# Prefix and suffix products by scans: reset by a maximum with a PSUM constant and four pad columns, in place of an added tile; the attention output moves to the first score bank

## The chip, the cores and the metric

One NeuronCore of a Trainium2 chip runs the whole kernel. The metric is the device time of one execution in microseconds (us); each run shown is one execution, and the median of several is compared. The engines are called as the profile calls them: PE (TensorE, matrix multiplication; PEld is its weight load), DVE (VectorE), ACT (ScalarE), POOL (GpSimd) and SP (SyncE, which issues the DMAs here). [...]

## The reference

A gated linear attention over 4 batches, 8 heads, 768 tokens and a head size of 48 feeds an MLP with a rational activation, 384 to 2048 to 384:

```python
for t in range(S):
    state = alpha[:, :, t, :, None] * state + einsum('bhd,bhe->bhde', k[:, :, t], v[:, :, t])
    y[:, :, t] = einsum('bhd,bhde->bhe', q[:, :, t], state)
...
h = x @ w_in                      # x: y with the heads joined, 3072 x 384
P = a[0] + a[1] * h + a[2] * h**2 + a[3] * h**3
Q = 1.0 + abs(b[0]) * abs(h) + abs(b[1]) * h**2
out = (P / (Q + 1e-06)) @ w_out
```

alpha is drawn between 0.8 and 1. All is float32, and matrix products in the later part of the kernel are split into a high and a low part (`gh` and `gl`, `hi` and `lo`).

## The kernel before

**Attention.** The tokens are cut into 24 chunks g of 128. Within a chunk the recurrence is turned into matrix products: k is multiplied by the product of all alphas after its token, q by the product of those up to it divided by the chunk's total. Both products come from DVE scans over a tile `ta` of shape 128 x 516: heads and channels on partitions, four groups side by side in the free dimension, each with one pad column and 128 tokens (`C1 = C + 1`). The step `suf` (line 404) runs backwards and gives `tg`, the step `pre` (line 419) runs forwards and gives `fp`. Each computes state = state * ta + second tile. The pad of `ta` is 0, which ends the group before; the second tile, 0 but in the pads, adds the start value of the next group: a constant 1 in `ones1` for `suf`, and in `d1` for `pre` the reciprocal of the chunk's total, which the steps `max` (line 409, clamps the total) and `inv` (line 416) put there just before. Both scans so read two SBUF tiles of 516 columns.

```python
nc.vector.tensor_tensor_scan(
    fp[g % 2], ta[g % 2][:, 0 : NC4 * C1], d1, 0.0, op0=ALU.mult, op1=ALU.add
)
```

Steps of one chunk, in the names of the order table: `ta`, `tk`, `tq` (DVE transposes of alpha, k and q into place; the first four chunks come by PE transposes `tn` and ACT copies `cp` instead), `suf`, `max`, `inv`, `pre`, `k` and `q` (multiply by the products, lines 433 and 436), `tot` (totals per head for the state, line 424), `s` (scores on PE into PSUM banks 4 and 5, line 450), `se` and `sm` (ACT copy, POOL mask, lines 457 and 461), `kt` and `ke` (k transposed on PE into bank 4, ACT copy), `d` (decay of the state, line 474), `am` (on PE: y into bank 3, and the new k-v products into bank 5, lines 492 and 511), `kv` (state update on DVE, lines 519 and 524), `xh` and `xl` (y out of its bank as a high part by ACT, line 538, and a low part by DVE, line 543).

**MLP.** Blocks m of 256 tokens, and for each 8 slices of 256 hidden columns: 96 units u in all, of which the first 16 run in plain float32 while the weights are still being joined and split. A unit is: `in` twice (PE, line 571 or 577, into bank u % 3), ACT `ah`, `t1`, `q1`, POOL `qm` (line 593), DVE `t2`, `t3` (lines 604, 608), ACT `ars`, `sq` (lines 611, 614), DVE `p`, `t`, `g` (lines 618, 621, 627; with `g` the bank is free), ACT `gh`, then `gl` (line 634, on POOL or DVE), and `oh` twice and `ol` (PE, lines 652 and 662, into banks 6 and 7). Weight steps early in the run: `abs` on ACT, `sign` (lines 246 and 248), `low`, `join` on DVE, `hi` on ACT, `lo` (line 286, DVE or POOL).

**What sets the order.** All steps are registered with `add(name, engine, cost, function, arguments, after, ...)`. The order in which they are issued is written out in the table `ORDER`, a compressed list of step numbers, one order for all engines together. Where a step has an `alt`, the high bit of its number says that the alternative engine runs it. The costs do nothing when the kernel is built. The waits between engines follow from what the steps read and write.

**PSUM banks.** 0 to 2: hidden units. 3: y (`bank(3)` in `attn_mm`, `x_hi`, `x_lo`, and the verdict at the end). 4 and 5: scores, transposed k, k-v products. 6 and 7: the output. Before the first units the banks also hold the transposed first inputs (`NAT_BANKS`).

A step at the end sums up whether any alpha lies outside 0.75 to 1.05; only then would a general path (`general`) run, which doesn't run with these inputs.

Of the kernel before, what the change touches and what calls it, by code (L numbers as in the profile page):

```python
# [22 lines left out]
class Plan:  # L23
# [85 lines left out]
    'h>7!P|oM~-F<oA+PCnTp@OgLI|lXqC|}W!b1i)@Khd@EqkUiB({~7KB>jAE-`2Nr^?e`T&bRjs{czVQ=;+3}2EK!@8P?',
    'wq@B{rA-^h>k-GVv3u^;Dqxj}w{pXlfMj()rk@mZj=Z|m0iP(R6ccb!Ib@$-B;H`!-{`924Xa#Q?NA2y<^U+=TS0zb|7',  # L110
    '@EiOh-z8Y=7y7||iSO+W_@#cMAL5t!>HeVK<g>z1pA$y-fo{1U=4bd7{*d3|2ZiN=t$wCI?8mrEezR{MHq;&Q+x#rQ-L',
    'LdV{VJauj``z$w!iFm_?`ZQF95rI9ysYw`PIG)gt^oHiXY&f_%%MnO>)=#NPouf_E-H=zt&&(dq&*w&;2uh(}%iO{+2)',
    'MyTUiW*XM(M{=3f)dEvJ28NBeX{T+YK7lfbwuD|DB`u*PP8-L#a@W1>YKh^#9Z@uaTUkEPx!ERdEegDpXk<qR&bc6T)w',
    '}0Tf!w~n-htm%}kv{T?^*{g58-47pPIpdw1rap7M${66Kl&n&ML&(`5k%6@KC6E5ph+~cM$xan7(~?>E}3=@qG@s^o$Z',
    'opbY(3LF*Jpy)Kr>UapV-2U1Mr76-}dQHJujM*qTeTX${Sxxi!!@8cS<xPA#EvwWN-Bv%=DA86EEPXkM+Q`LvYg*LYeK',
    'GH3#=ttFw3meq_}S_^1BEvPeH@1T{|)l6DQ%V}#Z1?3>Kme=~)Kzl%GXsCs?tya*AT1h)-5pAO#wVn3SqFPzYKqGCeeY',
    'L%I(k9wjt7uj2r~P%bcG0fdRLep&9i#)af6z_GXoz;#u{uzz>s$@hFl{z+jvKE%p~uMPS{?@LI31!xwHM6OiP}PkX-l1',
    ';y<ve4*DbnGC+QMhq&;=AZq;78SeNP)-KNWQx%SqnI!*fo)Ag9H&=I;rkLyZJsM~dyj?~>cLwD*-U8Q?;ua44vdQxxbY',
    'CWT8^@PsSn>t(P=zcw*r}UN1*IT+qPwQH}t@refp40PsU+?Ncy`Zo4fnL-%x=tVJdcCCa^^qPLxj{GSA3dz^^sipl$NE',
    'ICjC`yA=?6Wc|1@IoUXSWWHGvBv1)ub@La<qF@KnDj29blS`c=Pazu=lu@NDFF<>0zT4K}I-iGwJ?b4?QX;DtsDk_H-N',  # L120
    '4Wb7xHAWCK_@S|aY(eZGSr8{k8T{1bK@j}X6hV&Qx8@2`1v!J%L7E_LkUNMMgbVTn;e)(EzF=UGHb@u557GzugA74|pk',
    'NRo7!dRg3Iz#*!a>F$VUQ@u6l4yv1Vu)L1Vw{lLGd6o2n$LDrGxB2iJ)ZgKP+N&Ed',
# [13 lines left out]
    (0, "a"): (0, 1), (0, "k"): (2, 3), (0, "q"): (6, 7),  # L136
# [4 lines left out]
GB = 3  # L141
# [13 lines left out]
def tile_gla_then_rational_mlp(ctx, tc, q, k, v, alpha, w_in, w_out, ca, cb, out):  # L155
# [34 lines left out]
    def bank(n, cols=BANK):  # L190
        return ps[:, n * BANK : n * BANK + cols]
# [104 lines left out]
    C1 = C + 1  # L296
# [15 lines left out]
    st_d = work.tile([P, H * D], F32, name="st_d")  # L312
# [6 lines left out]
    def set_ta(s):  # L319
        nc.gpsimd.memset(ta[s][:, 0 : NC4 * C1 + 1 : C1], 0.0)  # L320

    def set_d1():
        nc.gpsimd.memset(d1, 0.0)
# [677 lines left out]
```

## Time and profile before

| | |
|---|---|
| median of 3 runs | 573.96 us (573.42 to 574.5) |
| the profiled execution | 574.5 us |
| its span, first to last instruction | 572.8 us |
| mean granted clock of PE | 0.993 |
| instructions | 13516 |
| DVE scans | 48 in two lines, 24 each |

In the lines of the profile, L404 is line 404 of the kernel; an entry such as `x24: 1204/1226/2378` is a count and the shortest, median and longest duration in ns; `| 18.9, 1889 |` is busy time in us and mean duration in ns. A wait is written with who waited, for whom, the total in us, how often and the longest. Durations of an engine's instructions may overlap by a little, so busy time is a union and not the sum.

### The profile page before, as it was taken

The numbers are of one execution on the slowest core, as the hardware profiler recorded it, in microseconds if no ns is written. First come the engines' busy times: TensorE is split into PE (matmuls) and PEld (weight loads), VectorE is DVE, ScalarE is ACT, GpSimd is POOL, SyncE is SP. The second block draws the span as 40 slices with busy tenths as digits, with TensorE's granted clock in tenths as the row PEclk, the third lists the DMA queues.
The fourth block names the chain that finished last, engine by engine and source line by source line (L and its number), as shares of the span: only waits on it lengthen the run. The fifth ranks groups of instructions, "written<-read, shape, count | busy, mean of one in ns | idle before, by whom it ended". The sixth has DMA issues, their size and how long they took to land.

```text
span 572.8 us, 13516 instructions
## 1 busy us (share of the span) xinstructions
PE 533.6 (93%) x5170; PEld 480.9 (84%) x5170; DVE 523.5 (91%) x767; ACT 457.5 (80%) x773; POOL 351.6 (61%) x316
## 2 busy tenths in 40 slices
PE   5888999889999999999899999999999999999995
PEld 4766666666798999899799999998999899999894
DVE  3999999999999999999899999899898999888883
ACT  2667776657897887987799898988888888898893
POOL 3257368757787776767479576665665565564351
PEclk9989999999999999999999999999999999999998
DMA  9978735355654452235434342543153120020001
GB/s 263 302 214 221 216 76 145 85 148 134 155 154 118 104 142 60 50 92 121 108 85 118 90 98 62 121 103 89 43 128 87 40 68 1 1 80 2 28 1 33
DMA packets 120550, 59.94 MB, mean 105 GB/s; under 512 B 101792, under 2 KB 113056, under 8 KB 120480
## 3 DMA queue, kind: packets, MB, share of 16 engines
q1 hardware_dynamic: 120480, 59.02, 39.9%
q8 instruction: 42, 0.69, 0.5%
q14 instruction: 28, 0.23, 0.1%
HBM read 47.98 MB, written 4.72 MB: 92 GB/s over the span
## 4 chain that ended last, share of the span: by engine, by line
DVE 30%; PE 29%; ACT 13%; DMA 10%; SPq 9%; issue 7%; POOL 2%; DVEq 0%; ACTq 0%
PE ps L577 12%; PE ps L652 7%; SPq L354 7%; PE ps L662 4%; DVE t L604 4%; DVE t L608 4%; DVE ps L621 3%; DVE t L618 3%; DMA wo_words<-in_moe_w_out_dram 3%; DVE t L627 3%; DMA raw_k<-in_k_dram 2%; DMA raw_a<-in_alpha_dram 2%; ACT ps L611 2%; DVE tg L404 2%; ACT ps L614 2%
## 5 line engine op out<-in xcount | busy, mean ns | idle before, releaser
L577 PE MATMUL ps<-x,wi 128*128 128x256 f32 x1440 | 199.6, 284 | 8.3 <-DVE t L627 6.7
L577 PEld LDWEIGHTS ps<-x,wi 128*128 128x128 f32 x1440 | 187.2, 189 | 18.0 <-DVE t L627 12.6
L593 POOL TENSOR_TENSOR qm<-qm,ah 128x512 f32<-128x512 f32 x96 | 131.5, 1371 | 107.6 <-ACT qm L590 102.4
L652 PE MATMUL ps<-wo,gh 128*128 128x384 f32 x640 | 136.0, 343 | 1.0 <-ACT gh L630 0.7
L652 PEld LDWEIGHTS ps<-wo,gh 128*128 128x128 f32 x640 | 105.9, 188 | 4.4 <-ACT gh L630 1.6
L634 POOL TENSOR_TENSOR gl<-t,gh 128x512 fp32r<-128x512 f32 x58 | 77.3, 1333 | 49.4 <-ACT gh L630 33.0
L611 ACT ACTIVATE ps<-qm,one_eps 128x512 f32<-128x512 f32 x96 | 66.2, 689 | 32.4 <-DVE t L608 21.1
L618 DVE SCALAR_TENSOR_TENSOR t<-t,coef,ps 128x512 f32<-128x512 f32 x96 | 70.6, 736 | 15.6 <-ACT ps L614 15.0
L590 ACT ACTIVATE qm<-ah,bab 128x512 f32<-128x512 f32 x96 | 77.9, 813 | 6.7 <-DVE ps L621 5.7
L587 ACT ACTIVATE t<-ps,coef 128x512 f32<-128x512 f32 x96 | 74.2, 772 | 9.7 <-PE ps L577 3.2
L584 ACT ACTIVATE ah<-ps 128x512 f32<-128x512 f32 x96 | 56.8, 593 | 25.4 <-PE ps L577 8.9
L608 DVE SCALAR_TENSOR_TENSOR t<-t,coef,ps 128x512 f32<-128x512 f32 x96 | 70.6, 737 | 3.3 <-ACT ah L584 1.9
L604 DVE TENSOR_TENSOR t<-t,ps 128x512 f32<-128x512 f32 x96 | 64.7, 675 | 7.7 <-ACT t L587 5.1
L662 PE MATMUL ps<-wo,gl 128*128 128x384 f32 x320 | 69.7, 340 | 0.9 <-DVE gl L634 0.9
L627 DVE SCALAR_TENSOR_TENSOR t<-ps,t 128x512 f32<-128x512 f32 x96 | 65.7, 684 | 1.8
L621 DVE SCALAR_TENSOR_TENSOR ps<-qm,ps 128x512 f32<-128x512 f32 x96 | 65.8, 685 | 0.1
L614 ACT ACTIVATE ps<-ps 128x512 f32<-128x512 f32 x96 | 56.1, 584 | 1.8
L662 PEld LDWEIGHTS ps<-wo,gl 128*128 128x128 f32 x320 | 53.4, 188 | 1.6 <-DVE gl L634 1.1
L630 ACT ACTIVATE gh<-t 128x512 fp32r<-128x512 f32 x80 | 50.1, 628 | 5.0 <-DVE t L627 4.7
L571 PE MATMUL ps<-x,wi_words 128*128 128x256 f32 x192 | 47.8, 392 | 5.9 <-DVE t L627 5.5
L571 PEld LDWEIGHTS ps<-x,wi_words 128*128 128x128 f32 x192 | 36.2, 194 | 16.7 <-DVE t L627 8.7
L645 PE MATMUL ps<-wo_words,t 128*128 128x384 f32 x128 | 46.8, 490 | 1.2 <-DVE t L627 1.2
(97 smaller groups left out, 732.2 us busy)
## 6 DMA issues: line engine op xcount, KB each, us to landing
raw_a<-in_alpha_dram SPq DMA_DIRECT2D x160, 48.0 KB, 2.1
raw_k<-in_k_dram SPq DMA_DIRECT2D x160, 48.0 KB, 2.1
raw_q<-in_q_dram SPq DMA_DIRECT2D x160, 48.0 KB, 2.1
wi_words<-in_moe_w_in_dram SPq DMA_DIRECT2D x8, 768.0 KB, 6.3
wo_words<-in_moe_w_out_dram SPq DMA_DIRECT2D x8, 768.0 KB, 7.5
tv<-in_v_dram SPq DMA_DIRECT2D x24, 192.0 KB, 3.2
out_dram<-parts SPq DMA_DIRECT2D x24, 192.0 KB, 2.3
wr<-in_alpha_dram SPq DMA_DIRECT2D x18, 256.0 KB, 3.0
```

The lines of the kernel that those rows point to most:

```text
L571: nc.tensor.matmul(h, whole(("i", j))[:, kt * FU + ff, :], x[:, kt, 0, :], start=(kt == 0), stop=(kt == KT - 1),)
L577: nc.tensor.matmul(h, w(("i", j))[:, kt * FU + ff, :], x[:, kt, xp, :], start=(kt == 0 and n == 0), stop=(kt == KT - 1 and n == 2),)
L590: nc.scalar.activation(buf(s, "qm", u), buf(s, "ah", u), AF.Identity, bias=b0, scale=b1)
L593: nc.gpsimd.tensor_tensor(buf(s, "qm", u), buf(s, "qm", u), buf(s, "ah", u), op=ALU.mult)
L604: nc.vector.tensor_tensor(t, t, h_of(u), op=ALU.mult)
L608: nc.vector.scalar_tensor_tensor(t, t, a1, h_of(u), op0=ALU.add, op1=ALU.mult)
L611: nc.scalar.activation(h_of(u), buf(s, "qm", u), AF.Abs_reciprocal_sqrt, bias=one_eps)
L618: nc.vector.scalar_tensor_tensor(t, t, a0, h_of(u), op0=ALU.add, op1=ALU.mult)
L621: nc.vector.scalar_tensor_tensor(h_of(u), buf(s, "qm", u), 1.0 + 1e-6, h_of(u), op0=ALU.add, op1=ALU.mult)
L627: nc.vector.scalar_tensor_tensor(t, h_of(u), 2.0, t, op0=ALU.subtract, op1=ALU.mult)
L652: nc.tensor.matmul(o_of(tt), buf(s, "gh", u)[:, ff, tt * P : (tt + 1) * P], w(("o", j))[:, ff, :], start=(j == j0 and ff == 0 and w is hi) ...
L662: nc.tensor.matmul(o_of(tt), buf(s, "gl", u)[:, ff, tt * P : (tt + 1) * P], hi(("o", j))[:, ff, :], start=False, stop=(j == j1 and ff == F ...
```

## The change

The scans no longer add a second tile; they take the maximum with one constant: state = max(state * ta, FLOOR) with FLOOR = 2^-55. The constant is one PSUM column of bank 3, broadcast over the columns. Between two groups there now stand four pad columns (`PAD = 4`, so 528 columns for 516). In `ta` the pads are 2^55, 0, 2^55 and a last one: the 0 brings the state down to FLOOR, the 2^55 next to it brings it to 1, and the last pad, which `inv` fills with the reciprocal of the total, makes it the start value for `pre`. `max` writes to PSUM (`least_p`), `inv` reads it there and writes into `ta`; `max` now runs on DVE only and is ordered after the `inv` of the chunk before, where it was ordered after the `pre`. `totals` reads its two halves from PSUM where DVE runs it. The tiles `d1` and `ones1` and their fills on POOL go; a DVE fill of bank 3 (`set_consts`) and more pad fills in `set_ta` come.

Bank 3 thereby is taken by constants. y moves to bank 4 (`SCB`), the first score bank, so that `s` of a chunk is ordered after `xh` and `xl` of the chunk before; the verdict moves there too; k of the first block is transposed into banks 4 and 5, where it was 2 and 3.

The order table is a new one. Read out step by step, its counts by engine are these (the steps whose engine changes beside others that stay):

| step | before, DVE / POOL | after, DVE / POOL |
|---|---|---|
| `max` | 4 / 20 | 24 / 0 |
| `tot` | 5 / 15 | 11 / 9 |
| `gl` | 22 / 58 | 14 / 66 |
| `k` | 4 / 20 | 2 / 22 |
| `q` | 5 / 19 | 3 / 21 |
| `lo` | 5 / 11 | 2 / 14 |
| `sign` | 12 / 4 | 11 / 5 |
| `d` | 4 / 16 | 4 / 16, four others each way |

PE, ACT and SP run the same steps as before, in another order.

```diff
-    (0, "a"): (0, 1), (0, "k"): (2, 3), (0, "q"): (6, 7),
+    (0, "a"): (0, 1), (0, "k"): (4, 5), (0, "q"): (6, 7),
...
-    C1 = C + 1
+    PAD = 4
+    C1 = C + PAD
+    FLOOR = 2.0 ** -55
...
-    d1 = work.tile([P, NC4 * C1], F32, name="d1")
...
-    ones1 = work.tile([P, NC4 * C1], F32, name="ones1")
+    CB = 3 * BANK
+    floor_p = ps[:, CB : CB + 1]
+    halves_p = ps[:, CB + 8 : CB + 10]
+    least_p = ps[:, CB + 16 : CB + 16 + NC4]
...
     def set_ta(s):
-        nc.gpsimd.memset(ta[s][:, 0 : NC4 * C1 + 1 : C1], 0.0)
...
+        pads = ta[s][:, 0 : NC4 * C1].rearrange("p (a t) -> p a t", t=C1)
+        nc.gpsimd.memset(pads[:, :, 0:3], 1.0 / FLOOR)
+        nc.gpsimd.memset(pads[:, :, 1:2], 0.0)
+        nc.gpsimd.memset(pads[:, :, 3:4], 1.0)
+        nc.gpsimd.memset(ta[s][:, NC4 * C1 :], 1.0)
+
+    def set_consts():
+        nc.vector.memset(bank(3), FLOOR)
+        nc.vector.tensor_copy(halves_p, halves)
...
     def suffix(g):
         nc.vector.tensor_tensor_scan(
-            tg[g % NTG][:, ::-1], ta[g % 2][:, 1:][:, ::-1], ones1, 0.0, op0=ALU.mult, op1=ALU.add
+            tg[g % NTG][:, ::-1], ta[g % 2][:, 1:][:, ::-1], floor_p.to_broadcast([P, NC4 * C1]), 1.0,
+            op0=ALU.mult, op1=ALU.max,
         )
...
+    def least(g):
+        nc.vector.tensor_scalar(least_p, totals_of(g), FLOOR, 2.0 ** 100, op0=ALU.max, op1=ALU.min)
 
     def inverse(g):
-        t = d1[:, 0 : NC4 * C1 : C1]
-        nc.vector.reciprocal(t, t)
+        nc.vector.reciprocal(ta[g % 2][:, PAD - 1 : NC4 * C1 : C1], least_p)
 
     def prefix(g):
         nc.vector.tensor_tensor_scan(
-            fp[g % 2], ta[g % 2][:, 0 : NC4 * C1], d1, 0.0, op0=ALU.mult, op1=ALU.add
+            fp[g % 2], ta[g % 2][:, 0 : NC4 * C1], floor_p.to_broadcast([P, NC4 * C1]), 1.0,
+            op0=ALU.mult, op1=ALU.max,
         )
...
     def attn_mm(g):
         sc, vt, kt = scs[g % NSC], tv[g % 3], kts[g % NSC]
-        y = bank(3)
+        y = bank(SCB)
...
-        add(("max", g), "DVE", 0.2, least, (g,),
-            [("suf", g), ("pre", g - 1), "d1"], lock=True, alt=("POOL", 0.35, False))
+        add(("max", g), "DVE", 0.2, least, (g,), [("suf", g), ("inv", g - 1)])
...
-        add(("s", g), "PE", SV[0], sc_mm, (g,), [("k", g), ("q", g), ("se", g - 1), ("kv", g - 1), ("ke", g - 1), ("am", g - 1)] + near, lat=0.13)
+        add(("s", g), "PE", SV[0], sc_mm, (g,), [("k", g), ("q", g), ("se", g - 1), ("kv", g - 1), ("ke", g - 1), ("am", g - 1), ("xh", g - 1), ("xl", g - 1)] + near, lat=0.13)
```

More of the change, by code (lines that the diff above doesn't have):

```diff
@@ L123 @@
+    '{Tgy4wUAYyPu|LQw+!9V?|pLCu+(a&lE2)^i5eX7^=t6~s2px~P(3ZeziG*XZ_7!*8L4kU;YL=SwhNuvf?f*8RIjTwB`',
+    'Btfh|M<ori2FZfhLGmC)kTOW1IfCrL56v0m3Vv#;;Frb;HfZV~cMvzo6XXrj1o?t^K@fxs(gx{*@Im|_e~>;%5EKX!1_',
+    'gtRL53hxkU1z66bT9kMT25N@gQ3e5|j)|1ffBx;D3>QXrT',
 ]
@@ L379, in turned @@
         if nm == "a":
-            return ta[g % 2][:, 1:].rearrange("p (a t) -> p a t", t=C1)[:, :, 0:C]
+            return ta[g % 2][:, 0 : NC4 * C1].rearrange("p (a t) -> p a t", t=C1)[:, :, PAD:]
         return (tk if nm == "k" else tq)[g % NQ]
@@ L404, in suffix, with totals_of @@
         nc.vector.tensor_tensor_scan(
-            tg[g % NTG][:, ::-1], ta[g % 2][:, 1:][:, ::-1], ones1, 0.0, op0=ALU.mult, op1=ALU.add
-        )
-    def least(eng, g):
-        eng.tensor_scalar(
-            d1[:, 0 : NC4 * C1 : C1], tg[g % NTG][:, 0 : NC4 * C1 : C1], 2.0 ** -60, 2.0 ** 100,
-            op0=ALU.max, op1=ALU.min,
-        )
+            tg[g % NTG][:, ::-1], ta[g % 2][:, 1:][:, ::-1], floor_p.to_broadcast([P, NC4 * C1]), 1.0,
+            op0=ALU.mult, op1=ALU.max,
+        )
+    def totals_of(g):
+        return tg[g % NTG][:, PAD - 1 : NC4 * C1 : C1]
+    def least(g):
+        nc.vector.tensor_scalar(least_p, totals_of(g), FLOOR, 2.0 ** 100, op0=ALU.max, op1=ALU.min)
     def inverse(g):
-        t = d1[:, 0 : NC4 * C1 : C1]
-        nc.vector.reciprocal(t, t)
+        nc.vector.reciprocal(ta[g % 2][:, PAD - 1 : NC4 * C1 : C1], least_p)
     def prefix(g):
         nc.vector.tensor_tensor_scan(
-            fp[g % 2], ta[g % 2][:, 0 : NC4 * C1], d1, 0.0, op0=ALU.mult, op1=ALU.add
+            fp[g % 2], ta[g % 2][:, 0 : NC4 * C1], floor_p.to_broadcast([P, NC4 * C1]), 1.0,
+            op0=ALU.mult, op1=ALU.max,
         )
@@ L424, in totals @@
         eng.tensor_tensor(
-            tot[g % NQ], tg[g % NTG][:, 0 : NC4 * C1 : C1].unsqueeze(2).to_broadcast([P, NC4, 2]),
-            halves.unsqueeze(1).to_broadcast([P, NC4, 2]), op=ALU.mult,
+            tot[g % NQ], totals_of(g).unsqueeze(2).to_broadcast([P, NC4, 2]),
+            (halves if eng is nc.gpsimd else halves_p).unsqueeze(1).to_broadcast([P, NC4, 2]), op=ALU.mult,
         )
     def after_pad(t):
-        return t.rearrange("p (c t) -> p c t", t=C1)[:, :, 1:]
+        return t.rearrange("p (c t) -> p c t", t=C1)[:, :, PAD:]
     def mult_k(eng, g):
@@ L537, in x_hi @@
         o = x_of(m)[:, :, 0, cc * C : (cc + 1) * C]
-        nc.scalar.activation(o, bank(3, DM).rearrange("p (k t) -> p k t", t=C), AF.Copy)
+        nc.scalar.activation(o, bank(SCB, DM).rearrange("p (k t) -> p k t", t=C), AF.Copy)
     def x_lo(g):
@@ L543, in x_lo @@
         nc.vector.tensor_tensor(
-            x_of(m)[:, :, 1, cs], bank(3, DM).rearrange("p (k t) -> p k t", t=C),
+            x_of(m)[:, :, 1, cs], bank(SCB, DM).rearrange("p (k t) -> p k t", t=C),
             x_of(m)[:, :, 0, cs].bitcast(F32), op=ALU.subtract,
@@ L704, in verdict_mm @@
     def verdict_mm():
-        nc.tensor.matmul(ps[0:1, 3 * BANK : 3 * BANK + 1], vd_tot, vd_ones, start=True, stop=True)
+        nc.tensor.matmul(ps[0:1, SCB * BANK : SCB * BANK + 1], vd_tot, vd_ones, start=True, stop=True)
     def verdict_ok():
-        nc.vector.tensor_scalar(ok, ps[0:1, 3 * BANK : 3 * BANK + 1], 0.0, None, op0=ALU.is_equal)
+        nc.vector.tensor_scalar(ok, ps[0:1, SCB * BANK : SCB * BANK + 1], 0.0, None, op0=ALU.is_equal)
     def general():
@@ L765, in general @@
                     nc.sync.dma_start(xn, xd[:, tok, :].rearrange("h t e -> t h e"))
-                    xp = bank(3, DM)
+                    xp = bank(SCB, DM)
                     for kt in range(KT):
@@ L814, in tile_gla_then_rational_mlp @@
         add(("set", "ta", s), "POOL", 0.1, set_ta, (s,))
-    add("d1", "POOL", 0.5, set_d1)
-    add("ones1", "POOL", 0.6, set_ones)
     for s in range(3):
@@ L819, in tile_gla_then_rational_mlp @@
     add("halves", "POOL", 0.4, set_halves)
+    add("consts", "DVE", 0.8, set_consts, (), ["halves"])
     add("set_st", "POOL", 0.6, set_st)
@@ L864, in tile_gla_then_rational_mlp @@
                 ready[nm] = [("t" + nm, g)]
-        add(("suf", g), "DVE", 1.25, suffix, (g,), ready["a"] + ["ones1", ("k", g - NTG), ("tot", g - NTG), ("max", g - NTG)], lock=True)
-        add(("max", g), "DVE", 0.2, least, (g,),
-            [("suf", g), ("pre", g - 1), "d1"], lock=True, alt=("POOL", 0.35, False))
+        add(("suf", g), "DVE", 1.25, suffix, (g,), ready["a"] + ["consts", ("k", g - NTG), ("tot", g - NTG), ("max", g - NTG)])
+        add(("max", g), "DVE", 0.2, least, (g,), [("suf", g), ("inv", g - 1)])
         add(("inv", g), "DVE", 0.18, inverse, (g,), [("max", g)])
-        add(("pre", g), "DVE", 1.25, prefix, (g,), [("inv", g), ("q", g - 2)], lock=True)
+        add(("pre", g), "DVE", 1.25, prefix, (g,), [("inv", g), ("q", g - 2)])
         add(("k", g), "POOL", 1.22, mult_k, (g,), [("suf", g)] + ready["k"], alt=("DVE", 0.69, True))
@@ L872, in tile_gla_then_rational_mlp @@
         if not first(g):
-            add(("tot", g), "POOL", 0.24, totals, (g,), [("suf", g), "halves", ("d", g - NQ)], alt=("DVE", 0.15, True))
+            add(("tot", g), "POOL", 0.24, totals, (g,), [("suf", g), "halves", "consts", ("d", g - NQ)], alt=("DVE", 0.15, False))
         add(("v", g), "SP", DMA, load_v, (g,), [("set", "v", g % 3), ("am", g - 3)], kb=1.2)
```

129 lines of the change are left out of this document (60 added, 69 removed).

## The prediction

> **What bounds the kernel now.** I read the page's first two parts, then a table by stretches, then who waits for whom in each stretch.
>
> ```profile
> PE 533.6 (93%) x5170; PEld 480.9 (84%) x5170; DVE 523.5 (91%) x767; ACT 457.5 (80%) x773; POOL 351.6 (61%) x316
> ...
> PE   5888999889999999999899999999999999999995
> ...
> DVE  3999999999999999999899999899898999888883
> ```
>
> Two engines are over 90%, so the average doesn't say which one sets the time. The digits do: VectorE (DVE) is full from the second slice to about the sixteenth, TensorE (PE) is not; later it is the other way round. The borders I take are 20, 220 and 540 us.
>
> ```profile
> core 0: us, PE busy (x) PEld busy (x) DVE busy (x) ACT busy (x) POOL busy (x), PEclk, DMA share, GB/s
> ...
> 20.00:220.00 200.00, 183.70 (x1734) 149.29 (x1732) 196.59 (x278) 149.90 (x237) 137.37 (x104) 0.99 0.56 149
> 220.00:540.00 320.00, 311.92 (x3197) 295.98 (x3185) 294.79 (x444) 277.04 (x485) 197.15 (x172) 1.00 0.30 73
> ```
>
> In the first stretch DVE has 3.4 us idle of 200 and PE 16.3: DVE bounds it. In the second PE has 8.1 idle of 320 and DVE 25.2: PE bounds it. After 540 there are no scans (their last starts stand below). The waits of PE agree, first for 20 to 220, then for 220 to 540:
>
> ```profile
> PE ps L571 <- DVE t L627: 5.5, 5, 2.5
> PE ps L450 <- POOL tk L433: 2.6, 1, 2.6
> ...
> PE ps L577 <- DVE t L627: 1.6, 3, 0.7
> PE ps L645 <- DVE t L627: 1.2, 1, 1.2
> ...
> PE ps L492 <- DVE x L543: 0.7, 1, 0.7
> ...
> PE ps L450 <- DVE st_s L519: 0.2, 1, 0.2
> ```
>
> ```profile
> PE ps L577 <- DVE t L627: 5.1, 9, 1.0
> PE ps L662 <- DVE gl L634: 0.9, 1, 0.9
> PE ps L450 <- DVE tq L436: 0.8, 1, 0.8
> ```
>
> The columns are us in total, times, longest. L627 is g, the last DVE step of a unit; PE waits for it 8.3 us in the first stretch, and for DVE 6.8 us in the second.
>
> **The change, part by part.**
>
> *The scans.* Before, both read two SBUF tensors (ta and an added tile). Each scan's length (min/median/max):
>
> ```profile
> L404 DVE TENSOR_TENSOR_SCAN tg<-ta,ones x24: 1204/1226/2378, 11.2 to 476.6; 128x516 f32<-128x516 f32 x24
> ```
>
> ```profile
> L419 DVE TENSOR_TENSOR_SCAN fp<-ta,d x24: 1208/1346/2853, 14.6 to 486.0; 128x516 f32<-128x516 f32 x24
> ```
>
> ```profile
> L618 DVE SCALAR_TENSOR_TENSOR t<-t,coef,ps x96: 697/742/756, 42.7 to 560.5; 128x512 f32<-128x512 f32 x96
> ```
>
> The same scan takes 1.2 us or up to 2.85. The timeline shows with what:
>
> ```profile
> 268.43 1.30 POOL L634 TENSOR_TENSOR gl<-t,gh 128x512 fp32r<-128x512 f32 x1
> 268.45 2.38 DVE L404 TENSOR_TENSOR_SCAN tg<-ta,ones 128x516 f32<-128x516 f32 x1
> ...
> 269.68 2.04 POOL L461 TENSOR_SCALAR_AFFINE_SELECT sc<-sc 128x1024 f32<-128x1024 f32 x1
> ```
>
> The scan that begins 0.02 us after a GpSimd (POOL) operation ends about 1.1 us later than its undisturbed 1.2 us would, and the POOL operation that begins under the scan takes 2.04 us and ends 0.9 us after it. So a two-SBUF-input scan and a POOL operation exclude each other. L618 reads one tensor from SBUF and one from PSUM, runs 96 times beside the same POOL work, and never exceeds 756 ns. The new scans have that kind of inputs (ta, and one PSUM constant), so I expect them never to be held and never to hold POOL.
>
> How long is a free one? A wider scan, 528 elements for 516, adds 1226 x 12/516 = 28 ns at most. That its second input is in PSUM and has a step of zero, and that the second operation is a maximum, no row shows. The nearest are two 512-element products, with a PSUM input and without:
>
> ```profile
> L604 DVE TENSOR_TENSOR t<-t,ps x96: 636/677/690, 38.1 to 557.0; 128x512 f32<-128x512 f32 x96
> ```
>
> ```profile
> L433 DVE TENSOR_TENSOR tk<-tk,tg x4: 682/688/693, 13.8 to 279.1; 128x512 f32<-128x512 f32 x4
> ```
>
> PSUM is 11 ns cheaper there, so the lower end is minus 11. For the step of zero: L474, quoted below, reads both inputs so and takes 565 ns for 384 elements, against 677 x 384/512 = 508, which is 57 more, or 78 at 528 elements. Of minus 11 and plus 78 I take none, since L604 is the row nearest to a PSUM input: 1.25 us a scan; the ends are -0.5 and +3.7 us over 48 scans. [...]
>
> *DVE in the first stretch.* The groups of 20 to 220 us (count | busy, mean ns):
>
> ```profile
> L419 DVE TENSOR_TENSOR_SCAN fp<-ta,d 128x516 f32<-128x516 f32 x10 | 18.9, 1889 | 0.0
> L404 DVE TENSOR_TENSOR_SCAN tg<-ta,ones 128x516 f32<-128x516 f32 x9 | 11.9, 1337 | 0.0
> ...
> L248 DVE TENSOR_SCALAR wo_words<-wo_words 128x768 uint32<-128x768 uint32 x5 | 4.5, 903 | 0.0
> ...
> L286 DVE TENSOR_TENSOR wi<-wr,wi 128x768 fp32r<-128x768 f32 x3 | 4.0, 1345 | 0.0
> L634 DVE TENSOR_TENSOR gl<-t,gh 128x512 fp32r<-128x512 f32 x3 | 3.1, 1024 | 0.0
> ...
> L286 DVE TENSOR_TENSOR wo<-wr,wo 128x768 fp32r<-128x768 f32 x2 | 1.9, 951 | 0.1
> L474 DVE TENSOR_TENSOR st_d<-st_s,tot 128x384 f32<-128x384 f32 x3 | 1.7, 565 | 0.0
> L416 DVE RECIPROCAL d<-d 128x4 f32<-128x4 f32 x9 | 1.5, 166 | 0.0
> L436 DVE TENSOR_TENSOR tq<-tq,fp 128x512 f32<-128x512 f32 x1 | 1.4, 1394 | 0.0
> L409 DVE TENSOR_SCALAR d<-tg 128x4 f32<-128x4 f32 x3 | 1.1, 355 | 0.0
> ```
>
> Scans: 18.9 + 11.9 = 30.8 us for 19, against 19 x 1.25 = 23.8: 7.0 saved. The steps that the new order table moves between DVE and POOL, up to unit 28, where this stretch ends: lo, four off and one on, 3 x 1.19 (5.9/5) = 3.6 saved; gl, three off and one on, 2 x 1.02 = 2.0; one sign 0.9; one q 1.4; d, three off, 3 x 0.57 = 1.7. On to DVE come eight max, priced as the reciprocal, the row nearest to four elements, 8 x 0.17 = 1.3; the three that stay lose their blocking, 3 x (0.355 - 0.17) = 0.6 saved; three more totals (eight elements) at the same price 0.5. Net of the moves: 3.6 + 2.0 + 0.9 + 1.4 + 1.7 + 0.6 - 1.3 - 0.5 = 8.4. With the scans DVE loses 15.4 us of 196.6.
>
> How much of it reaches the end? PE has 16.3 idle there, so it can follow, but only by becoming nearly full. POOL takes what DVE gives up:
>
> ```profile
> L634 POOL TENSOR_TENSOR gl<-t,gh 128x512 fp32r<-128x512 f32 x9 | 12.8, 1427 | 4.9 <-ACT gh L630 3.0 <-issue 1.1 <-POOL st_d L474 0.7
> L436 POOL TENSOR_TENSOR tq<-tq,fp 128x512 f32<-128x512 f32 x9 | 12.6, 1397 | 4.8 <-ACT tk L393 3.5 <-DVE fp L419 1.3
> L286 POOL TENSOR_TENSOR wo<-wr,wo 128x768 fp32r<-128x768 f32 x6 | 11.9, 1985 | 4.4 <-ACT wo L281 4.4
> L246 POOL TENSOR_SCALAR wo_words<-wo_words 128x768 f32<-128x768 f32 x3 | 6.9, 2289 | 0.4 <-ACT parts L241 0.3
> L474 POOL TENSOR_TENSOR st_d<-st_s,tot 128x384 f32<-128x384 f32 x5 | 5.0, 993 | 0.1
> L409 POOL TENSOR_SCALAR d<-tg 128x4 f32<-128x4 f32 x6 | 3.6, 597 | 3.8 <-DVE tg L404 2.3 <-DVE fp L419 1.2
> ```
>
> lo 3 x 1.99, gl 2 x 1.43, sign 2.3, q 1.4, d 3 x 0.99, less six max of 0.6: 12.0 more, 149 of some 188 us, or 79%. POOL isn't the bound, but its queue is in order and qm of every unit stands in it, behind two-microsecond pieces. Also, max leaves POOL, where it waited 3.5 us for scans with qm behind it; on DVE it waits for nothing on another engine. I take 12 of the 15.4, the rest lost to PE and POOL queues that no longer have slack.
>
> *Second stretch.* Its scans and gl get shorter too, but PE bounds it. Only PE's 6.8 us of waits for DVE can go; I take 3, because the moved order can free a bank earlier only where the waiting unit's other inputs are there.
>
> *Costed at nothing.* Set-up: two tile fills leave POOL, pad fills and a DVE fill of bank 3 come, all under the first load of alpha, for which PE waits longest of all:
>
> ```profile
> PE ps L374 <- DMA raw_a<-in_alpha_dram: 6.9, 1, 6.9
> ```
>
> If that cover is missing the fill costs DVE one 512-element operation, 0.68 (L604). No DMA is added or taken away; SP's loads are only reordered, and the q, k and alpha loads still wait for the same transposes. Bank 4 for y: s(g), the next scores, now waits for both copies of y out of the bank (xh on ScalarE, xl on DVE). Counted in the new order, from chunk 4 on at least four PE steps stand between am(g-1) and s(g), and xl stands near kv(g-1), for which s(g) waited already. So nothing, with the first rival as its price. Natural k turned into banks 4 and 5, not 2 and 3: first scores wait for those copies, which they read anyway.
>
> Sum against the profiled execution, 574.5 us (span 572.8 and 1.7 around it): 574.5 - 12 - 3 = 559.5. That execution is 0.5 above the median of the runs, 573.96, so 559.0.
>
> **Rivals.** *Slower: y's copies become the wait.* s(g) stands in PE's queue ahead of matmuls of the MLP; if xl, queued on DVE, is late, all of them wait. 20 chunks have an xl. It decides from 15/20 = 0.75 us per chunk beyond the cover; with 1.2 us, 24 lost against 15 gained, 583. For it: DVE is full. Against: the four steps, and that before 220 us PE's one wait at the scores for the kv step (L519) was 0.2 us, and its one at L492 for xl (L543) 0.7. [...]
>
> *PE takes over sooner.* Only the 8.3 us of PE's waits for g shrink, by a half, and 1 in the second stretch: 5 in all, 569. For it: the other 8 of PE's idle time have other names.
>
> *More.* All 16.3 and 6.8 us go: 23, 551. For it: POOL operations get shorter as well.
>
> *The change does not do what it says.* A scan fed from PSUM excludes POOL all the same. Then the moves' 8.4 remain, of which 12/15.4 passes, 6.5, less 48 x 0.028 = 1.3 for wider scans: 569. Against: L618.
>
> **How the numbers follow.** Forecast 0.64 (554 to 565), PE sooner 0.14 (565 to 574), more 0.10 (546 to 554), slower by y 0.08 (575 to 590), no exclusion lifted 0.04 (565 to 576). 549 to 570 leaves out the slower case, some of PE sooner, and the ends of the others, 0.18; the scans' ends (-0.5 to +3.7) lie inside. About 0.2%, 1.15 us, is what a measurement tells from no change. Faster: 0.64 + 0.10 + 0.10 of PE sooner + 0.02 of the last: 0.86; same 0.03 + 0.01; slower 0.08 + 0.01 + 0.01.
>
> **What would show it.** Scans at 1.2 to 1.3 us without a tail, for both lines; no POOL operation lengthened under one; all 48 together near 60 us; the full digits of DVE end some 12 us earlier; PE's 8.3 us of waits for g mostly gone. Wrong: scans above 1.35, PE waiting at the scores (L450) for DVE x, or POOL above 85% in the first stretch with ScalarE waiting for qm.

## The result and the profile after

The changed kernel takes 569.18 us (median of 4 runs, 568.74 to 569.49), against 573.96 us for the kernel before, run beside it; a fourth run of the kernel before took 2951 us and is left out of its median. The ratio is 0.9916 with the interval 0.9897 to 0.9936: faster by 5 us. The forecast was 15 us. The time lies inside the range, close to its upper end; the sign is right and the size is three times too large.

The first two parts of the page of the kernel after, cut to the rows shown of before:

```profile
span 567.2 us, 13536 instructions
...
PE 532.4 (94%) x5170; PEld 484.5 (85%) x5170; DVE 500.2 (88%) x779; ACT 459.3 (81%) x773; POOL 348.3 (61%) x309
...
PE   5878999999999999999999999999999899999983
...
DVE  4989999999999899999998899998898989986781
```

DVE lost 23.3 us of busy time (523.5 before), far more than the span lost (5.6). Beside one 8 in the third slice, its first digit below 9 now stands in the fourteenth slice (from 184 us), where it stood in the twentieth (from 272 us); the prediction looked for some 12 us between them. The profiled execution took 568.9 us.

The scans, now lines 409 and 424 (minimum, median, maximum in ns):

```profile
L409 DVE TENSOR_TENSOR_SCAN tg<-ta,ps x24: 1215/1244/1255, 11.3 to 454.3; 128x528 f32<-128x528 f32 x24
```

```profile
L424 DVE TENSOR_TENSOR_SCAN fp<-ta,ps x24: 1207/1246/1255, 14.5 to 480.3; 128x528 f32<-128x528 f32 x24
```

The tail is gone: the longest of 48 takes 1255 ns, where one of before took 2853 and 20 took over 1300, each of these beside a POOL operation. 41 of the 48 run beside a POOL operation for a part of their time, and none of them is lengthened; the seven without one take 1235 to 1254 ns. As groups (busy us, mean ns | idle before):

```profile
L424 DVE TENSOR_TENSOR_SCAN fp<-ta,ps 128x528 f32<-128x528 f32 x24 | 29.8, 1242 | 0.2
L409 DVE TENSOR_TENSOR_SCAN tg<-ta,ps 128x528 f32<-128x528 f32 x24 | 29.8, 1240 | 2.4 <-ACT ta L398 2.3
```

All 48 take 59.6 us; the forecast was 60.

Where the time came from is seen best between the same points of the work. The steps of a unit end with g on DVE (L627 before, L633 after). Its execution for unit 28 stands below, first before, then after (durations in ns, start in us):

```profile
L627 DVE SCALAR_TENSOR_TENSOR t<-ps,t x1: 653/653/653, 218.9 to 218.9; 128x512 f32<-128x512 f32 x1
```

```profile
L633 DVE SCALAR_TENSOR_TENSOR t<-ps,t x1: 691/691/691, 210.8 to 210.8; 128x512 f32<-128x512 f32 x1
```

Unit 28 ends at 219.6 before and at 211.5 after, 8.1 us sooner. In the same way unit 8 ends at 99.1 and 98.6, and unit 92 at 550.8 and 542.9. So, by these points, 0.5 us were won up to unit 8, 7.6 from there to unit 28, and nothing in the 64 units after it. The tables by stretches, cut at these points, first before:

```profile
20.00:99.10 79.10, 70.08 (x628) 52.97 (x626) 77.27 (x107) 55.90 (x87) 47.65 (x35) 0.98 0.66 185
99.10:219.60 120.50, 113.21 (x1074) 95.92 (x1078) 118.92 (x172) 93.61 (x150) 89.71 (x70) 1.00 0.50 127
20.00:219.60 199.60, 183.30 (x1702) 148.89 (x1704) 196.19 (x278) 149.50 (x237) 137.37 (x104) 0.99 0.56 150
```

Then after (columns as in the prediction: length, then busy time and count of PE, PEld, DVE, ACT, POOL):

```profile
20.00:98.60 78.60, 68.61 (x612) 51.28 (x610) 75.25 (x105) 56.47 (x88) 45.60 (x34) 0.98 0.67 198
98.60:211.50 112.90, 111.13 (x1109) 95.80 (x1110) 106.61 (x174) 93.15 (x148) 89.14 (x71) 1.00 0.51 131
20.00:211.50 191.50, 179.74 (x1721) 147.07 (x1720) 181.87 (x278) 149.62 (x235) 134.75 (x104) 0.99 0.57 159
```

For 278 instructions in either kernel (not all the same ones) DVE needs 196.19 - 181.87 = 14.3 us less: the forecast of 15.4 for what DVE loses was close. But 12.3 of it lies between units 8 and 28, and there PE was idle for only 120.50 - 113.21 = 7.3 us. After the change it is idle for 1.8: PE is full, the stretch is 7.6 shorter, and DVE now stands idle for 6.3. Up to unit 8 PE's idle time stayed (9.0 before, 10.0 after).

The orders differ, so at the end of the same unit PE has not always done the same work in both kernels. Between units 8 and 28 it ran 96 and 44 output matmuls of the high and the low part before, and 88 and 40 after: one unit's outputs lie on the other side of the border. PE's idle time fell by 5.5 us there, and the rest of the 7.6 is a difference of its busy time. At the ends of units 40 and 86 PE has finished the same matmuls in both, by kind too. The tables with borders there and at unit 92, first before:

```profile
20.00:286.50 266.50, 246.65 (x2358) 207.84 (x2356) 258.47 (x370) 204.65 (x333) 178.71 (x139) 0.99 0.52 134
286.50:525.70 239.20, 235.52 (x2464) 224.60 (x2464) 222.20 (x337) 210.21 (x368) 149.38 (x133) 1.00 0.30 73
525.70:550.80 25.10, 24.24 (x173) 23.55 (x172) 20.98 (x32) 22.16 (x39) 9.80 (x8) 1.00 0.05 17
```

Then after:

```profile
20.00:275.90 255.90, 243.81 (x2358) 208.40 (x2356) 242.40 (x374) 206.90 (x337) 177.62 (x139) 0.99 0.55 146
275.90:515.70 239.80, 236.92 (x2464) 227.53 (x2464) 215.45 (x344) 211.01 (x370) 145.60 (x120) 1.00 0.28 69
515.70:542.90 27.20, 24.85 (x172) 23.76 (x172) 20.91 (x34) 22.52 (x38) 10.28 (x9) 1.00 0.06 23
```

At unit 40 the change is 10.6 us ahead: PE is idle for 12.1 us since 20 us where it was for 19.9, and busy for 2.8 us less with the same matmuls, which is not explained. From unit 40 to 86 nothing is won, with PE 98.5% busy before and 98.8% after. From unit 86 to 92 2.1 us are lost; PE waits for g there for 2.3 us, before for 0.9.

In the first stretch PE's waits for g went from 8.3 us to 3.7, all of them before 100 us. But its wait for the copy of the scores, at the transposes of k, 2.0 us before, is now its longest there; the waiter, for whom, the total in us, how often and the longest, from 20 to 220 us after the change:

```profile
PE ps L474 <- ACT sc L463: 4.5, 2, 3.2
PE ps L577 <- DVE t L633: 2.2, 2, 1.3
PE ps L651 <- DVE t L633: 1.5, 1, 1.5
```

From 220 to 540 us after the change PE has two waits in its list:

```profile
PE ps L583 <- DVE t L633: 3.5, 5, 1.4
PE ps L658 <- ACT parts L680: 0.5, 1, 0.5
```

The wait for g is 5.1 us in before's list and 3.5 here, and still unit 28 to unit 92 takes 331.2 us before and 331.4 after. PE waits less and is no sooner done. Behind the last matmul, before takes 6.9 us to the end of the span and after 8.8. This gives back 1.9 us, and the way from unit 92 to the last matmul 0.4, so that 7.9 at unit 92 become 5.6. Only the last copies and stores, the branch around `general` and the closing waits between the engines stand there; SP's closing wait for PE takes 2.0 us where it took 0.6.

### The profile page after: what moved, and what is told of

The parts are those of the page before. It is cut to its first block, busy times and chain, and to the rows that moved or that the text cites. A ratio compares the mean times of both kernels' runs of the same rounds, so it can differ in the third digit from the quotient of the medians.

```text
span 567.2 us, 13536 instructions
## 1 busy us (share of the span) xinstructions
PE 532.4 (94%) x5170; PEld 484.5 (85%) x5170; DVE 500.2 (88%) x779; ACT 459.3 (81%) x773; POOL 348.3 (61%) x309
## 4 chain that ended last, share of the span: by engine, by line
PE 47%; DVE 19%; DMA 8%; SPq 8%; ACT 8%; issue 6%; POOL 4%; DVEq 0%; POOLq 0%; ACTq 0%
PE ps L583 18%; PE ps L658 13%; PE ps L668 6%; SPq L359 4%; PE ps L498 4%; DMA wi_words<-in_moe_w_in_dram 3%; DVE t L624 3%; DVE t L633 3%; DVE ps L627 2%; DVE t L610 2%; PE ps L456 2%; DMA wo_words<-in_moe_w_out_dram 2%; DVE t L614 2%; ACT ah L590 2%; PE ps L577 1%
## 5 line engine op out<-in xcount | busy, mean ns | idle before, releaser
L583 PEld LDWEIGHTS ps<-x,wi 128*128 128x128 f32 x1440 | 190.2, 188 | 11.1 <-DVE t L633 8.6
L599 POOL TENSOR_TENSOR qm<-qm,ah 128x512 f32<-128x512 f32 x96 | 126.1, 1314 | 115.5 <-ACT qm L596 113.8
L640 POOL TENSOR_TENSOR gl<-t,gh 128x512 fp32r<-128x512 f32 x66 | 86.1, 1305 | 52.3 <-ACT gh L636 36.8
L593 ACT ACTIVATE t<-ps,coef 128x512 f32<-128x512 f32 x96 | 74.3, 775 | 15.4 <-PE ps L583 7.2
L633 DVE SCALAR_TENSOR_TENSOR t<-ps,t 128x512 f32<-128x512 f32 x96 | 66.0, 688 | 2.0
L627 DVE SCALAR_TENSOR_TENSOR ps<-qm,ps 128x512 f32<-128x512 f32 x96 | 65.9, 686 | 0.0
L651 PE MATMUL ps<-wo_words,t 128*128 128x384 f32 x128 | 48.3, 502 | 1.6 <-DVE t L633 1.5
```

What stands on the lines that cost most here:

```text
L583: nc.tensor.matmul(h, w(("i", j))[:, kt * FU + ff, :], x[:, kt, xp, :], start=(kt == 0 and n == 0), stop=(kt == KT - 1 and n == 2),)
L599: nc.gpsimd.tensor_tensor(buf(s, "qm", u), buf(s, "qm", u), buf(s, "ah", u), op=ALU.mult)
L627: nc.vector.scalar_tensor_tensor(h_of(u), buf(s, "qm", u), 1.0 + 1e-6, h_of(u), op0=ALU.add, op1=ALU.mult)
L633: nc.vector.scalar_tensor_tensor(t, h_of(u), 2.0, t, op0=ALU.subtract, op1=ALU.mult)
L640: eng.tensor_tensor(buf(s, "gl", u).rearrange("p a b -> p (a b)"), buf(s, "t1", u), gh, op=ALU.subtract)
```

## The experiments

Each is an edit of the kernel after unless it says otherwise; each ratio is against the kernel before, run on the same chip. The theory is that PE's idle time sets the gain; the rivals differ by experiment.

**The constant in SBUF.** The scans keep their new form and order, but the floor is an SBUF column.

```diff
-    floor_p = ps[:, CB : CB + 1]
+    floor_t = work.tile([P, 1], F32, name="floor")
+    floor_p = floor_t
...
+        nc.vector.memset(floor_t, FLOOR)
```

> The changed kernel with one edit: the scans' constant lies in an SBUF tile of one column instead of a PSUM column, so each scan again has two SBUF inputs. Order, pads, maximum and y's bank stay. Theory (PSUM as second input takes the scans out of the exclusion with GpSimd, and that gives most of the gain): scans again get a tail over 2 us and a mean of 1.4 to 1.65 us (1.24 in the changed kernel), DVE busy 510 to 520 us (500.2), time 573 to 578 us. Rival (the new order and the moved steps give the gain, the scans' inputs do not matter): scans 1.24 us or, if longer, without effect on the end, time 569 to 570.5.

Measured: 584.11 us, ratio 1.0169 (1.0146 to 1.0191), 15 us above the kernel after, and above the theory's span. The tail is back, by this one edit:

```profile
L411 DVE TENSOR_TENSOR_SCAN tg<-ta,floor x24: 1227/1401/2834, 11.5 to 469.9; 128x528 f32<-128x528 f32 x24
```

```profile
L426 DVE TENSOR_TENSOR_SCAN fp<-ta,floor x24: 1245/1742/2343, 14.4 to 495.9; 128x528 f32<-128x528 f32 x24
```

A scan of one tensor and one broadcast column, both in SBUF, is held just as the scan of two tensors was: 33 of the 48 take over 1300 ns, and all 33 run beside a POOL operation. So it is the constant in PSUM that frees the scans, and in the new order it is worth 15 us, more than before and after differ by. A part of that may be PE's granted clock, which was 0.980 to 0.994 in these runs and 0.989 to 0.991 after; the run at 0.994 took 582.67 us. The new order is no better in itself: with held scans it is 10 us worse than the kernel before.

**The new scans in the old order.** The table of before, with `max` on DVE and 21 of the steps `xh`, `xl` and the last copies moved ahead where the shared bank needs it.

```diff
-ORDER = [   (the new table)
+ORDER = [   (the table of before, with the 21 steps moved ahead)
```

> The changed kernel's scans, pads, constants and banks in the old order of steps, with the old choice between DVE and GpSimd (max on DVE, as it must be); 21 copies of y (xh, xl) and their like are issued a few steps earlier, since y's new bank needs it. Theory (the scans' freedom between 100 and 220 us is what counts, 6.6 us of blocking there, and PE's idle time of 7.3 us there is the limit): 567 to 571 us. Rival (the moves of lo, gl, d, sign to GpSimd are needed): 573 to 576 us.

Measured: 578.67 us, ratio 1.0076 (1.0063 to 1.0088), above what both theories expected. PE waits at the scores (L455) for y's low part:

```profile
PE ps L455 <- DVE x L548: 12.4, 12, 3.6
```

This is the first rival of the prediction, by its own name. It isn't among PE's waits in the new order, but it is real in the old one.

**The same with y's low part off the bank.** To price that wait, `xl` reads the constant bank, so that the scores wait for `xh` alone; the low part of y is left out.

```diff
-            x_of(m)[:, :, 1, cs], bank(SCB, DM).rearrange("p (k t) -> p k t", t=C),
-            x_of(m)[:, :, 0, cs].bitcast(F32), op=ALU.subtract,
+            x_of(m)[:, :, 1, cs], bank(3, DM).rearrange("p (k t) -> p k t", t=C),
+            x_of(m)[:, :, 0, cs].bitcast(F32), op=ALU.mult,
```

> The new scans in the old order (578.7 us), with one edit: xl, the low-part copy of y on DVE, reads the constant bank and not y's bank, so that the next scores wait for xh alone; the low part of y is left out. Theory (PE's 12.4 us of waits at the scores for xl, in the old order, are what makes that version slow): 564 to 571 us. Rival (something else of the old order, such as max on DVE or the unmoved lo, gl and d): 575 to 579 us.

Measured: 572.04 us, ratio 0.9962 (0.9944 to 0.9979), 6.6 us below the run before it and just above the theory's span; its runs scatter from 569.37 to 574.76. What is left of the wait has another name:

```profile
PE ps L455 <- ACT x L543: 6.2, 6, 3.0
```

**And in the new order, as a control.** The same two lines changed in the kernel after.

> The control to the old order with xl freed: the same edit (xl reads the constant bank, the next scores wait for xh alone, the low part of y is left out) in the changed kernel with its own order. Theory (the new order keeps scores and y's copies apart, so y's bank costs it nothing): 568 to 571 us. Rival (y's bank costs the new order too, hidden in other waits): 4 to 8 us less, 561 to 565.

Measured: 569.28 us, ratio 0.9911 (0.9894 to 0.9928): unchanged. The wait for y's low part costs the new order nothing that can be measured, PE's list of waits has none at the scores for either copy of y there, and the 6.6 us are the old order's.

**Scans over half of the columns.** Both scans cover 264 of 528 columns; the rest is filled once.

```diff
-            fp[g % 2], ta[g % 2][:, 0 : NC4 * C1], floor_p.to_broadcast([P, NC4 * C1]), 1.0,
+            fp[g % 2][:, 0:HALF], ta[g % 2][:, 0:HALF], floor_p.to_broadcast([P, HALF]), 1.0,
```

> The changed kernel with every scan over 264 of its 528 columns; the other half of tg and fp holds a constant, so the products of half the heads are left out. DVE loses 48 x 0.55 = 26 us of work. Theory (from 100 us on PE is full, so only the nine scans before that count): 9 x 0.55 = 5 us at most, time 564 to 568.5. Rival (DVE still sets the time): 15 to 25 us less, 545 to 554.

Measured: 564.4 us, ratio 0.9821 (0.9807 to 0.9835). DVE is busy for 24.1 us less (500.2 to 476.1), 0.50 a scan, where 0.55 was an estimate that no row gives, and the time falls by 4.8: a further cut of scans hardly passes to the end, as the theory had it. The place is not the theory's, which took PE for full from 100 us on: 2.4 of the 4.4 us between the profiled executions lie between units 28 and 92.

**Half of the low part's output matmuls left out, after and before.** This was priced at 28 us of PE, in the units after the first 16: 160 matmuls at 0.175 us, an estimate. At 303.62 us of the trace of after, four of them in a row take 0.87 us, and the median of one is 0.337, so some 0.18 from one to the next. PE's busy time falls by 20.2 us after (532.4 to 512.2) and by 23.3 before (533.6 to 510.3).

```diff
-            for ff in range(FU):
-                nc.tensor.matmul(
-                    o_of(tt), buf(s, "gl", u)[:, ff, tt * P : (tt + 1) * P],
-                    hi(("o", j))[:, ff, :],
-                    start=False, stop=(j == j1 and ff == FU - 1),
-                )
+            nc.tensor.matmul(
+                o_of(tt), buf(s, "gl", u)[:, 1, tt * P : (tt + 1) * P],
+                hi(("o", j))[:, 1, :],
+                start=False, stop=(j == j1),
+            )
```

> The changed kernel with half of the low-part output matmuls (two of four per unit) left out, from the 17th unit on: PE loses 80 x 2 x 0.175 = 28 us of work, all of it after 150 us. Theory (PE is full from 100 us on in the changed kernel): 15 to 28 us less, 541 to 554. Rival (DVE or a chain over several engines still sets the time): less than 8 us less, 561 to 569.

> The kernel before with half of the low-part output matmuls left out, from the 17th unit on (28 us of PE work, as in the run on the changed kernel, which fell by 10.8 us). Theory (in the kernel before DVE sets more of the time, so a relief of PE helps it less, and the change would be worth more if PE were not in the way): 566 to 571 us, 8 to 12 above the changed kernel with the same cut (558.4). Rival (PE is the limit of both alike): 561 to 565 us, so that the distance stays near 5.

Measured: after with the cut 558.38 us, ratio 0.9719 (0.9705 to 0.9733), 10.8 less than without, which is between the spans of the theory and the rival; before with the cut 573.12 us, ratio 0.9977 (0.9968 to 0.9986), 1.1 less and above both spans. The two stand 14.7 us apart, their profiled executions 13.0 (that of before with the cut, 571.44, is the fastest of its ten). The four tables from the end of unit 28 to that of unit 92 show where; before, after, before with the cut, after with the cut:

```profile
219.60:550.80 331.20, 323.12 (x3299) 307.10 (x3292) 305.47 (x460) 287.52 (x503) 200.52 (x175) 1.00 0.30 72
```

```profile
211.50:542.90 331.40, 325.84 (x3274) 312.61 (x3273) 296.89 (x471) 290.80 (x509) 198.76 (x165) 1.00 0.30 73
```

```profile
220.10:548.10 328.00, 307.10 (x3166) 284.20 (x3153) 306.03 (x461) 287.45 (x503) 199.05 (x175) 1.00 0.29 72
```

```profile
211.10:533.60 322.50, 307.29 (x3138) 289.81 (x3137) 292.81 (x472) 289.88 (x509) 200.22 (x165) 1.00 0.32 75
```

Less DVE work alone gains nothing here (331.2 to 331.4), less PE work alone 3.2, both together 8.7. The new order and the border at unit 28 come with the change in either pair, so the two differences can be compared: 0.2 lost without the cut, 5.5 won with it. Before, PE and DVE were both bounds of the second stretch, one right behind the other: PE at 97.6% was not the one engine to relieve. With PE's load cut, the change is worth 5.5 us in this stretch (328.0 to 322.5) and 9.0 up to unit 28 (220.1 to 211.1); behind unit 92 it loses 1.5. That the sum is near the forecast's 15 is in part chance, since the parts are not the forecast's 3 and 12. With the cut PE waits for g again, which says that g, through DVE or the chain over ACT to it, stands close behind it; these are the first rows from 220 to 540 us, before and after with the cut:

```profile
PE ps L577 <- DVE t L627: 14.2, 21, 1.6
```

```profile
PE ps L583 <- DVE t L633: 11.1, 15, 2.2
```

**Both cuts at once** (the last two diffs together).

> Both cuts at once in the changed kernel: scans over half their columns (26 us of DVE work) and half of the low-part output matmuls (28 us of PE work). Alone they gave 4.8 and 10.8 us. Theory (PE and DVE bound in turn, so each cut alone runs into the other engine): more than the sum, 20 to 30 us less, 539 to 549. Rival (a third thing, such as ACT or the chain through the units, stands behind them): the sum or less, 553 to 560.

Measured: 553.6 us, ratio 0.9637 (0.9623 to 0.9651): 15.6 below the kernel after, and 4.8 + 10.8 = 15.6. This is the sum, as the rival said, and below the theory's gain. By place it looks otherwise. From the end of unit 28 to that of unit 92, with half of the scans and then with both cuts:

```profile
209.80:538.80 329.00, 325.13 (x3274) 312.77 (x3273) 283.52 (x471) 290.38 (x509) 199.07 (x165) 1.00 0.31 73
```

```profile
211.90:529.30 317.40, 305.91 (x3141) 290.01 (x3140) 280.38 (x471) 289.41 (x509) 199.21 (x165) 1.00 0.31 76
```

Against the 331.4 of the kernel after, the scans alone gain 2.4 here, the matmuls alone 8.9 and both 14.0, which is more than 11.3, as the theory said, but by far less than it asked. In the rest of the profiled executions the two gain 2.0 and 1.6 alone and 1.1 together. So the equal sum does not show that a third thing stands behind the two. With both cuts PE still waits for g above all (8.5 us from 220 to 540), while DVE is idle for 37.0 of the 317.4 us; the chain of steps through a unit would do that, but it was not tested.

**Less work on ACT.** The range test of alpha is left out, with its loads; DVE gets one fill in its place. ACT's busy time falls by 22.3 us (459.3 to 437.0), less than the 32 expected.

```diff
     def guard_load(n):
+        return
         nc.sync.dma_start(wr[n % WB][:, 0:GW].bitcast(F32), alpha_flat[:, n, :])
...
-        nc.scalar.activation(
-            gj, ga, AF.Relu, bias=lim[:, j : j + 1], scale=(-STEEP, STEEP)[j],
-            accum_out=beyond[:, 2 * n + j : 2 * n + j + 1],
-        )
+        return
```

> The changed kernel without the test of alpha's range: 36 ACT passes of 0.9 us and 18 loads are left out, so ACT loses 32 us of work, all after 150 us. Theory (PE and DVE set the time from 100 us on, ACT has slack): less than 3 us less, 566 to 570. Rival (ACT, 88% busy from 220 to 540 us, is part of the bound): 6 to 15 us less, 554 to 563.

Measured: 566.41 us, ratio 0.9866 (0.9852 to 0.9881), 2.8 less. Most of ACT's time there is slack, as the theory had it.

**Less work on DVE before 100 us.** `low` runs on 8 columns, and `join` leaves the low word out; this was counted as some 20 us of DVE, all before 110 us, and DVE's busy time falls by 19.3 (500.2 to 480.9).

```diff
-            word(key, 0), word(key, 0), 29, word(key, 1), op0=ALU.logical_shift_right, op1=ALU.bitwise_or
+            word(key, 0)[:, 0:8], word(key, 0)[:, 0:8], 29, word(key, 1)[:, 0:8],
+            op0=ALU.logical_shift_right, op1=ALU.bitwise_or
...
-        nc.vector.scalar_tensor_tensor(
-            o, wr[wr_slot(n)].rearrange("p (b n) -> p b n", n=w), 3,
-            word(key, 0).rearrange("p (b n) -> p b n", n=w),
-            op0=ALU.logical_shift_left, op1=ALU.bitwise_or,
+        nc.vector.tensor_scalar(
+            o, wr[wr_slot(n)].rearrange("p (b n) -> p b n", n=w), 3, None, op0=ALU.logical_shift_left
         )
```

> The changed kernel with most of DVE's weight work of the first 110 us left out: low works on 8 columns of 768, and join shifts one operand and adds no low word (the weights' signs and last bits are left out). DVE loses some 20 us of work before 110 us. Theory (DVE's weight steps set the first 100 us, where PE has 10.0 us idle of 80, and PE is full after): 4 to 9 us less, 560 to 565. Rival (the weights' arrival, by DMA and ACT's first pass, sets that stretch): less than 2 us less, 567 to 570.

Measured: 562.7 us, ratio 0.9809 (0.9794 to 0.9824), 6.5 less, as the theory had it. The tables by stretches:

```profile
20.00:100.00 80.00, 74.93 (x645) 56.51 (x644) 65.95 (x117) 60.71 (x94) 46.95 (x35) 0.98 0.70 205
100.00:220.00 120.00, 118.24 (x1180) 104.81 (x1180) 111.82 (x184) 101.45 (x164) 94.92 (x75) 1.00 0.53 137
```

From 20 to 100 us PE is now idle for 5.1, where it was for 9 to 10 in both kernels. So this idle time could be had, but from the weight steps, not from the scans (with half of the scans' columns it is 8.8); the units from 8 on all come about 6.7 us sooner.

**The sign steps on ACT.** Here work is moved and not left out: 11 steps `sign` go from DVE to ACT, then all 16. The copy does not keep the signs, so the time is that of the steps' place alone.

```diff
-            eng.tensor_scalar(w, w, 0x80000000, None, op0=ALU.bitwise_and)
+            nc.scalar.activation(w.bitcast(F32), w.bitcast(F32), AF.Copy, scale=0.0)
```

> A version, not a cut: the eleven sign steps that DVE runs in the changed kernel (7.8 us in all) are done by ACT as a copy scaled by zero, at the same places of the order. Theory (DVE's weight steps set the first 100 us): 2 to 5 us less, 564 to 567. Rival (ACT's first passes set it, or ACT's queue gets too long): no gain or a loss, 569 to 573.

> As the run before, and the five sign steps on GpSimd (2.4 us each, during which two-SBUF-input steps of DVE are held) go to ACT too. Theory (the holding of DVE's weight steps by GpSimd, 6.5 us between 20 and 100 us, counts as well): another 1 to 4 us less than the run before, 561 to 566. Rival (ACT's queue): 569 to 575.

Measured: 569.66 us, ratio 0.9929 (0.9916 to 0.9942), and 569.55 us, ratio 0.9924 (0.9911 to 0.9937): no gain from either, as the rivals had it. DVE's waits in the first of them, 20 to 100 us:

```profile
DVE wo_words L251 <- ACT wo_words L248: 4.9, 2, 2.7
DVE wi_words L251 <- ACT wi_words L248: 3.3, 2, 2.1
```

`low` waits 8.2 us for the moved step, which now stands in ACT's queue behind the units' work. What DVE saved (76.7 us busy in this stretch after, 69.8 here) it spends in waiting.

## Why the prediction was right and wrong

*Right: what the constant does.* The tail is gone, both lines stand at 1.25 us, and putting the constant into SBUF brings the tail back and costs 15 us.

*Right: the price of a scan.* It was put at 1.25 us, and the medians are 1244 and 1246 ns. The shortest ones take 1215 and 1207 ns from PSUM and 1227 and 1245 with the same form from SBUF, so these rows show no extra time for the PSUM column.

*Right: what DVE loses in the first stretch.* 14.3 us for 15.4.

*Wrong: "I take 12 of the 15.4".* This is the step that failed; it measured 8.1 at unit 28. "PE has 16.3 idle there, so it can follow" was read over 200 us as one stretch. 9.0 of the 16.3 lay before unit 8, where DVE is full of weight steps, the change took only 2.0 from it, and PE's idle time did not fall. The other 7.3 lay where DVE lost 12.3, and 5.5 of it went. The digits that the prediction shows have PE at 9 from the tenth slice on (129 us) but for one 8, with DVE still at 9 up to the nineteenth; the border at 220 us hid that. The rival "PE takes over sooner" named PE as the limit, and its 5 us came out, with a chance of 0.14. But that is in part luck: it took 4 us here and 1 behind, and the runs show 8.1 here and a loss behind. POOL's instructions do start in the order in which the program issues them, in both traces (316 and 309 records), but its queue, to which I put down the rest, does not show as the cause: POOL is busy for 134.75 us of 191.5, 70%, not the 79% worked out, since its operations became shorter too (`qm` takes 1517 ns before and 1358 after, mean from 20 to 220 us), and ACT waits for `qm` for 1.2 us in all from 20 us to unit 28, where it was 3.6.

*Wrong: "I take 3" in the second stretch.* From unit 28 to unit 92 it measured -0.2: 2.5 won up to unit 40, 2.7 lost behind it. PE's waits for DVE did shrink, and its idle time fell from 8.1 to 5.6, but its busy time rose by 2.7, in part because one unit's outputs moved across the border. The prediction's sentence that PE bounds it was itself only half of it: with the matmuls cut, PE is busy for 16.0 us less in this stretch (323.1 to 307.1), and 3.2 come out.

*Not in the sum: the end.* 1.9 us were lost behind the last matmul and 0.4 just ahead of it, and I had no term for them. Kernels of the new form vary behind the last matmul between 7.0 and 9.3 us, and what sets it was not tried.

*Right for this order, and only for it: y's bank at nothing.* The control shows nothing to gain from y's low part in the new order; in the old one the same dependence costs 6.6 us and more.

The sum as measured, by unit ends: 0.5 + 7.6 - 0.2 - 0.4 - 1.9 = 5.6, as by the span, and 5 by the medians. Of the 9.4 us between 15 and 5.6, 3.9 are the first term's, 3.2 the second's and 2.3 the end's.

## What to carry to other kernels

When work is taken from a full engine, cap the gain by the idle time of the next engine in just those tens of microseconds where the work is saved, not by its idle time over the whole stage. An engine at 97% is not shown to be the bound (PE at 97.6% here gave 3.2 us for 16.0 of its work): cut its work and see, and cut the other's too, because two engines side by side gave little one at a time here (less DVE work 331.2 to 331.4 us, less PE work 3.2 us, both 8.7). Where two kernels have different orders, compare them at points where the engine has done the same work: by unit 28 the lead is 8.1 us, by unit 40, with equal work, 10.6. An order written out by hand belongs to its durations and banks: new scans in the old order took 578.7 us, held scans in the new order 584.1, and only the pair gave 569.2.

## What the runs showed of the hardware

POOL's product with the scan's result became slower with the new layout of that result (groups 132 columns apart and starting at column 4, for 129 and 1); the two rows are before and after:

```profile
L433 POOL TENSOR_TENSOR tk<-tk,tg x20: 1172/1200/2162, 37.6 to 502.1; 128x512 f32<-128x512 f32 x20
```

```profile
L439 POOL TENSOR_TENSOR tk<-tk,tg x22: 1271/1292/1733, 13.2 to 473.3; 128x512 f32<-128x512 f32 x22
```

Its shortest time rose by 99 ns, though its longest fell with the holding. The new scans in the old order show it as well (1261 ns at the shortest), so it does not come with the order; spacing and start were not tried apart. The same product on DVE takes 687 ns after and 688 before. And a PSUM column read with a step of zero costs a scan nothing that the rows show (1215 and 1207 ns at the shortest, 1227 and 1245 from SBUF), while with the same column in SBUF a scan beside a POOL operation takes up to 1.6 us longer (2834 ns against 1227).
